# M = kv · wo in four 32-column strips on TensorE, in a linear-attention and MLP block

## The chip, the cores and the metric

One core of a Trainium2 chip. The metric is the time of one execution in device microseconds (us); a profiled execution also gives a trace, whose span is some 2 us shorter than the time (221.4 us for the 223.35 us of the profiled run before). On one core a run counts as slow when it is over 1.5% above the fastest of its kernel; ratios use fast runs only. The first run of the kernel before (255.02 us) is such an outlier; its other two are 223.43 and 223.21 us.

## The reference, cut to what matters

```python
# x: 2048 tokens x 640;  H = 32 heads of 20
xn  = layernorm(x)
q, k, v = split(xn @ wqkv)                       # per head
pq, pk = phi(q), phi(k)                          # phi(t) = (t + 1 if t > 0 else exp(t)) + 1e-6
kv  = einsum("bhsd,bhse->bhde", pk, v)           # 20 x 20 per head
num = einsum("bhqd,bhde->bhqe", pq, kv)
den = einsum("bhqd,bhd->bhq", pq, sum_s(pk)) + 1e-6
A   = (num / den) @ wo
B   = gelu(xn @ w1 + b1) @ w2 + b2
out = x + A + B
```

The kernel never forms `num`. It folds `kv` (block diagonal over heads, 640 x 640) into `wo` once, M = kv · wo, and then computes A as (pq / den) · M. The change is in the making of M.

## The kernel before

A small planner writes one instruction list per engine in program order and adds semaphore waits where a tile or a PSUM bank is written, read or reused. Its PSUM tensor (`ps` in the traces, which all matmuls shown here write to) is allocated and used as eight banks of 512 fp32 per partition; `take(n)` hands them out in a ring, so **who used a bank last decides what a group of matmuls waits for**.

```python
def take(n):                      # ring over the 8 PSUM banks; pairs start at an even bank
    b = ring[0]
    if n == 2 and b % 2: b += 1
    b %= 8
    ring[0] = (b + n) % 8
    return b
...
def z_step():                     # z = sum of phi(k); ZB = head mask times z, for the denominator
    ...                           # ten one-column matmuls, a copy to z_sb
    for j in range(DT):           # DT = 5
        Pl.ins(v, lambda e, j=j: e.tensor_scalar(ZB[:, j, :], bmask[:], z_sb[:, j:j + 1], None, ALU.mult), ...)

def kvt_step():                   # kv transposed, off-head entries masked to zero by VectorE
    for t in range(DT):
        b = take(1)
        ...
        Pl.ins(v, lambda e, b=b, t=t: e.tensor_tensor(
            out=KVT[:, t, e0[t]:e1[t]], in0=bank(b, 0, Wd[t]), in1=maskKV[t][:], op=ALU.mult), ...)

def m_step():
    for j in range(DT):
        b = take(2)
        fns = []
        for t in range(DT):
            for h in range(2):
                fns.append(lambda e, t=t, h=h, b=b, j=j: e.matmul(
                    bank(b + h, 0, HW), KVT[:, t, j:D:DT], Wo[:, t, h * HW:(h + 1) * HW],   # HW = 320
                    start=(t == 0), stop=(t == DT - 1)))
        Pl.ins("tensor", fns, reads=[r_KVT, r_Wo], writes=B_[b:b + 2])
        Pl.ins("scalar", lambda e, b=b, j=j: e.activation(halves(Msb[:, j, :]), pair(b), ACT.Copy), ...)

def den_step(c):                  # denominator of one chunk of 512 tokens
    b = take(1)
    ...                           # five matmuls ZB x PQ; then VectorE: add, reciprocal, five multiplies

q_chunk(0)                        # five units: five matmuls of 512 columns, exp on ScalarE, phi on VectorE
z_step()
kvt_step()
q_chunk(1)
m_step()
den_step(0)
q_chunk(2)
q_chunk(3)
...
for t in range(NT):               # 16 output tiles, with the other denominators in between
    out_tile(t)
```

Each of M's five groups (one per j) takes every fifth column of KVT, 128 in all, as the stationary operand, and multiplies it with five blocks of Wo in two halves of 320 columns: 10 matmuls. Most of each operand is zero. 32 of its 128 columns cover 160 channels, eight heads, whose values lie in only two of the five 128-row blocks of KVT.

Of the kernel before, what the change touches and what calls it, by code (L numbers as in the profile page):

```python
# [112 lines left out]
def bass_parallel_sum__linear_attn_block__dense_activation_gelu__prompt_kernel(  # L113
    nc: bass.Bass, A_x, A_wqkv, A_wo, B_x, B_w1, B_b1, B_w2, B_b2, out):
    Batch, S, D = A_x.shape
# [6 lines left out]
    DT = D // P  # L122
# [3 lines left out]
    HW = D // 2  # L126
# [10 lines left out]
    with contextlib.ExitStack() as es:  # L137
# [14 lines left out]
        KVT = W1f[:, DT * D:2 * DT * D].rearrange("p (k d) -> p k d", k=DT)  # L152
        Wqkv = sb("Wqkv", [P, DT, 3 * D], BF16)
        W2 = sb("W2", [P, JT, D], BF16)
        Wo = sb("Wo", [P, DT, D], BF16)
# [28 lines left out]
        def take(n):  # L184
            b = ring[0]
            if n == 2 and b % 2:
                b += 1
# [4 lines that stand above are left out]
        def bank(b, lo=0, hi=512):  # L192
            return ps[:, b * 512 + lo: b * 512 + hi]

        def pair(b):
            return ps[:, b * 512:(b + 2) * 512].rearrange("p (a n) -> p a n", a=2)[:, :, 0:HW]

        def halves(ap):
            return ap.rearrange("p (a n) -> p a n", a=2)
# [222 lines left out]
        for t in range(NT):  # L422
            b = take(2)
            fns = []
# [10 lines left out]
        for f in range(DT):  # L435
            b = take(2)
# [51 lines left out]
        def m_step():  # L488
            for j in range(DT):
                b = take(2)  # L490
                fns = []
                for t in range(DT):
                    for h in range(2):
                        fns.append(lambda e, t=t, h=h, b=b, j=j: e.matmul(  # L494
                            bank(b + h, 0, HW), KVT[:, t, j:D:DT], Wo[:, t, h * HW:(h + 1) * HW],
                            start=(t == 0), stop=(t == DT - 1)))
                Pl.ins("tensor", fns, reads=[r_KVT, r_Wo], writes=B_[b:b + 2])
                Pl.ins("scalar", lambda e, b=b, j=j: e.activation(halves(Msb[:, j, :]), pair(b), ACT.Copy),
                       reads=B_[b:b + 2], writes=[r_M[j], r_zsum, r_zhl])
# [25 lines left out]
# [5 lines that stand above are left out]
# [83 lines left out]
```

## Time and profile before

| | before |
|---|---|
| time, median (of the first three runs, the outlier included) | 223.43 us |
| span of the trace | 221.4 us |
| TensorE (PE) busy | 214.4 us, 97% |
| M: first matmul to the denominator's first | 6.79 us |
| denominator's first to first output tile | 12.3 us |
| first output tile to the end | 80.2 us |

A note on the denominator. In all of these traces this denominator has four matmul records, not five, and it is the first that has none: the four run on to the next q chunk without a gap. I take its start as 0.22 us (one 512-column matmul) before the first one recorded, here 129.19 - 0.22 = 128.97.

From the page of the profile: the span, busy times with shares and instruction counts, PE's busy share in 40 slices in tenths, its granted clock in tenths, and the chain that ended last by engine.

```profile
span 221.4 us, 3944 instructions
PE 214.4 (97%) x1603; PEld 148.6 (67%) x1612; DVE 125.8 (57%) x227; ACT 74.3 (34%) x140; POOL 41.7 (19%) x74
PE   7699999999999999999999999999999999999994
PEclk9999999999999999999999999999999999999999
PE 88%; DVE 5%; DMA 3%; SPq 1%; issue 1%; DVEq 0%
```

PE is the limit nearly everywhere (97% busy, 88% of the chain that ended last), at full clock (mean granted clock 1.000). The timeline of PE around M (start us, duration us, engine, line, operation, output <- inputs, shapes, count):

```profile
117.01 5.34 PE L460 MATMUL ps<-xnT,Wqkv 128*128 128x512 bf16 x24
122.19 6.96 PE L494 MATMUL ps<-Wo,W 128*128 128x320 bf16 x50
129.19 1.03 PE L504 MATMUL ps<-PQ,ZB 128*128 128x512 bf16 x4
130.06 10.95 PE L460 MATMUL ps<-xnT,Wqkv 128*128 128x512 bf16 x49
141.27 3.42 PE L548 MATMUL ps<-W,HG 128*128 128x320 bf16 x24 [0.26 <-DVE PQ L417]
```

M is the second row: 50 matmuls, one every 136 ns, with no pause. (Its 6.96 us include the 0.17 us by which the last matmul outlasts its spacing.)

VectorE (DVE) in the same stretch. L415 and L417 are the phi of the second q chunk, L507 and L509 the denominator:

```profile
120.12 0.28 DVE L415 TENSOR_SCALAR ek<-ek 128x512 bf16<-128x512 bf16 x1
...
124.50 0.69 DVE L417 SCALAR_TENSOR_TENSOR PQ<-ps,ek 128x512 bf16<-128x512 f32 x1
130.26 0.69 DVE L507 TENSOR_SCALAR den_sb<-ps 128x512 f32<-128x512 f32 x1 [5.07 <-PE ps L504]
130.98 3.35 DVE L509 RECIPROCAL rden<-den_sb 128x512 bf16<-128x512 f32 x1
```

VectorE finishes that phi at 125.19, late, one unit per us, and then idles 5.07 us.

### The profile page before, as it was taken

To read this page: it belongs to the slowest core of one execution; us is meant where nothing else is said; L and a number is where in the kernel's file an instruction comes from. 1 tells how busy PE (TensorE), PEld (TensorE's weight loads), DVE (VectorE), ACT (ScalarE), POOL (GpSimd) and SP (SyncE) were. 2 spreads that over 40 slices of the span, in tenths; PEclk is the share of its full clock that TensorE was granted. 3 is DMA by queue.
4 is the path that set the end of the run, shared out by engine and by line. 5 is a ranking of instruction groups with operands and counts; after the bars stand their busy time and mean duration, and the time that the engine had idled before them with its cause. 6 is when DMAs were issued, how large, how long until landed. Compare 5 with 4: busy or idle time off the path is not lost.

```text
span 221.4 us, 3944 instructions
## 1 busy us (share of the span) xinstructions
PE 214.4 (97%) x1603; PEld 148.6 (67%) x1612; DVE 125.8 (57%) x227; ACT 74.3 (34%) x140; POOL 41.7 (19%) x74
## 2 busy tenths in 40 slices
PE   7699999999999999999999999999999999999994
PEld 2489999544447777777665865567767776777773
DVE  2767778500004888899078549889929414811211
ACT  2378877566667555111254542600000000000000
POOL 2246554200000000000000000079993000000000
PEclk9999999999999999999999999999999999999999
DMA  5999960000000000000000000254520010010011
GB/s 156 340 363 364 362 233 0 1 3 0 0 0 0 3 0 3 0 0 3 0 0 1 3 0 0 66 173 119 170 70 30 30 60 32 0 62 30 30 46 47
DMA packets 13706, 15.50 MB, mean 70 GB/s; under 512 B 632, under 2 KB 13688, under 8 KB 13688
## 3 DMA queue, kind: packets, MB, share of 16 engines
q1 hardware_dynamic: 13688, 15.24, 21.1%
q8 instruction: 13, 0.21, 0.4%
q14 instruction: 5, 0.04, 0.1%
HBM read 12.62 MB, written 2.62 MB: 69 GB/s over the span
## 4 chain that ended last, share of the span: by engine, by line
PE 88%; DVE 5%; DMA 3%; SPq 1%; issue 1%; DVEq 0%
PE ps L548 33%; PE ps L350 23%; PE ps L438 10%; PE ps L427 10%; PE ps L460 5%; PE ps L494 3%; DMA xPK<-in_A_x_dram 3%; PE ps L504 2%; PE ps L334 2%; DVE PQ L417 2%; DVE rden L509 2%; DVE PQ L511 1%; SPq L235 1%; PE ps L480 1%; SPq L231 1%
## 5 line engine op out<-in xcount | busy, mean ns | idle before, releaser
L350 PE MATMUL ps<-xnT,W 128*128 128x128 bf16 (+2 forms) x447 | 54.8, 279 | 2.1 <-DVE xnT L342 1.9
L548 PE MATMUL ps<-W,HG 128*128 128x320 bf16 x384 | 54.9, 299 | 0.3 <-DVE PQ L417 0.3
L548 PEld LDWEIGHTS ps<-W,HG 128*128 128x128 bf16 x384 | 37.5, 98 | 15.7 <-issue 0.7
L350 PEld LDWEIGHTS ps<-xnT,W 128*128 128x128 bf16 x450 | 36.1, 98 | 17.1 <-DVE xnT L342 1.5
L354 ACT ACTIVATE HG<-ps,b1c 128x128 bf16<-128x128 f32 (+2 forms) x90 | 41.1, 489 | 18.9 <-PE ps L350 17.5
L520 POOL TENSOR_TENSOR xnT<-xnT,b2bc 128x640 bf16<-128x640 bf16 x16 | 22.6, 1448 | 102.1 <-DMA xnT<-in_A_x_dram 102.1
L554 DVE TENSOR_TENSOR out_sb<-ps,xnT 128x640 bf16<-128x640 f32 x15 | 12.3, 823 | 33.4 <-PE ps L548 31.6
L414 ACT ACTIVATE ek<-ps 128x512 bf16<-128x512 f32 (+1 forms) x36 | 23.2, 645 | 23.8 <-PE ps L427 9.2
L415 DVE TENSOR_SCALAR ek<-ek 128x512 bf16<-128x512 bf16 (+1 forms) x36 | 10.9, 304 | 30.7 <-ACT ek L414 29.5
L548 PE MATMUL ps<-Msb,PQ 128*128 128x320 bf16 x160 | 24.5, 299 | 0.0
L427 PE MATMUL ps<-Wqkv,xnT 128*128 128x320 bf16 x160 | 21.9, 299 | 0.0
L438 PE MATMUL ps<-xPK,xn_tm 128*128 128x320 bf16 x160 | 21.9, 299 | 0.0
L460 PE MATMUL ps<-xnT,Wqkv 128*128 128x512 bf16 x97 | 21.6, 379 | 0.2
L427 PEld LDWEIGHTS ps<-Wqkv,xnT 128*128 128x128 bf16 x160 | 15.7, 98 | 6.2
L548 PEld LDWEIGHTS ps<-Msb,PQ 128*128 128x128 bf16 x160 | 15.7, 98 | 6.1
L438 PEld LDWEIGHTS ps<-xPK,xn_tm 128*128 128x128 bf16 x160 | 15.7, 98 | 6.1
L460 PEld LDWEIGHTS ps<-xnT,Wqkv 128*128 128x128 bf16 x100 | 11.7, 117 | 9.5
L307 DVE BATCH_NORM_STATS2 stats<-xPK 128x6 f32<-128x320 bf16 x32 | 15.1, 471 | 4.4 <-DMA xPK<-in_A_x_dram 4.4
L417 DVE SCALAR_TENSOR_TENSOR PQ<-ps,ek 128x512 bf16<-128x512 f32 x20 | 13.8, 692 | 2.1
L417 DVE SCALAR_TENSOR_TENSOR xPK<-ps,ek 128x640 bf16<-128x640 f32 x16 | 13.2, 825 | 1.7
L509 DVE RECIPROCAL rden<-den_sb 128x512 bf16<-128x512 f32 x4 | 13.4, 3353 | 0.1
L511 DVE TENSOR_TENSOR PQ<-PQ,rden 128x512 bf16<-128x512 bf16 x20 | 12.2, 674 | 0.1
(50 smaller groups left out, 113.6 us busy)
## 6 DMA issues: line engine op xcount, KB each, us to landing
xnT<-in_A_x_dram SPq DMA_DIRECT2D x4, 640.0 KB, 4.4
Wqkv<-in_A_wqkv_dram SPq DMA_DIRECT2D x3, 800.0 KB, 12.0
out_dram<-out_sb SPq DMA_DIRECT2D x15, 160.0 KB, 1.8
W<-in_B_w_dram SPq DMA_DIRECT2D x4, 480.0 KB, 5.7
xPK<-in_A_x_dram SPq DMA_DIRECT2D x3, 640.0 KB, 8.6
W<-in_B_w_dram SPq DMA_DIRECT2D x1, 1920.0 KB, 14.2
Wo<-in_A_wo_dram SPq DMA_DIRECT2D x1, 800.0 KB, 10.7
xPK<-in_A_x_dram SPq DMA_DIRECT2D x4, 160.0 KB, 4.8
```

The costliest lines, as they stand in the source:

```text
L307: Pl.ins(v, lambda e: e.bn_stats(stats[:, s, 6 * h:6 * h + 6], x_in[:, t, h * HW:(h + 1) * HW]), reads=[r_x[t]], writes=[r_stats[s]])
L350: Pl.ins("tensor", [(lambda e, k=k: e.matmul(bank(b, 0, w), W1[:, k, jb * P:(jb + 1) * P], xnT[:, k, tok], start=(k == 0), stop=(k == DT - ...
L354: Pl.ins("scalar", lambda e: e.activation(HG[:, jb, tok], bank(b, 0, w), ACT.Gelu_apprx_tanh, bias=b1c[:, jb:jb + 1]), reads=[B_[b], r_b1c ...
L414: Pl.ins("scalar", lambda e: e.activation(e2, src, ACT.Exp), reads=br, writes=[r_ek[s]])
L417: Pl.ins(v, lambda e: e.scalar_tensor_tensor(out=d2, in0=src, scalar=0.0, in1=e2, op0=ALU.max, op1=ALU.add), reads=br + [r_ek[s]], writes= ...
L427: fns.append(lambda e, k=k, h=h, b=b, t=t: e.matmul(bank(b + h, 0, HW), xnT[:, k, t * P:(t + 1) * P], Wqkv[:, k, D + h * HW:D + (h + 1) * ...
L438: Pl.ins("tensor", [(lambda e, t=t, h=h, b=b, f=f: e.matmul(bank(b + h, 0, HW), xn_tm[:, t, f * P:(f + 1) * P], PK[:, t, h * HW:(h + 1) * ...
L460: Pl.ins("tensor", [(lambda e, k=k, j=j, b=b: e.matmul(bank(b), Wqkv[:, k, j:D:DT], xnT[:, k, cc], start=(k == 0), stop=(k == DT - 1))) fo ...
L509: Pl.ins(v, lambda e: e.reciprocal(rden[:], den_sb[:]), reads=[r_den], writes=[r_rden])
L511: Pl.ins(v, lambda e, j=j: e.tensor_tensor(out=PQ[:, j, cc], in0=PQ[:, j, cc], in1=rden[:], op=ALU.mult), reads=[r_rden, r_PQ[c][j]], writ ...
L520: Pl.ins(g, lambda e: e.tensor_tensor(out=x_res[:, t, :], in0=x_res[:, t, :], in1=b2bc[:], op=ALU.add), reads=[r_xr[t // CH], r_b2], write ...
L548: return lambda e: e.matmul(bank(b + h, 0, HW), seq[i][0], seq[i][1][:, h * HW:(h + 1) * HW], start=(i == 0), stop=(i == n - 1))
```

## The change

The intent is to skip the zero blocks. Each group is cut into four quarters q of 32 columns. A quarter needs only blocks q and q+1, and its output goes to its own strip of 32 PSUM partitions. The hope is that four matmuls, one for each strip, then run at once; no trace before the change shows that.

```diff
-                for t in range(DT):
-                    for h in range(2):
-                        fns.append(lambda e, t=t, h=h, b=b, j=j: e.matmul(
-                            bank(b + h, 0, HW), KVT[:, t, j:D:DT], Wo[:, t, h * HW:(h + 1) * HW],
-                            start=(t == 0), stop=(t == DT - 1)))
+                for h in range(2):
+                    for i in range(2):
+                        for q in range(4):
+                            c0 = j + 32 * DT * q
+                            fns.append(lambda e, t=q + i, q=q, i=i, h=h, b=b, c0=c0: e.matmul(
+                                bank(b + h, 0, HW)[32 * q:32 * q + 32, :],
+                                KVT[:, t, c0:c0 + 31 * DT + 1:DT], Wo[:, t, h * HW:(h + 1) * HW],
+                                start=(i == 0), stop=(i == 1)))
```

That is 80 matmuls in place of 50, each with 320 moving columns. Everything else stays, in the same order on every engine.

## The prediction

> **What bounds the kernel now.** TensorE: busy 214.4 of 221.4 us (97%), full clock throughout (the page, parts 1 and 2), and 88% of the chain that ended last is PE (part 4). M is one stretch of that chain: 50 matmuls of 320 columns, 122.35 to 129.14 us, 6.79 us, 136 ns each. So at most 6.8 us (3.0%) can be won.
>
> **What the change does.** Each of the five M groups (one per j) has 16 matmuls with a 32-column stationary operand instead of 10 with 128 columns: 80 instead of 50, all of 320 moving columns. One by one at 136 ns, M would take 10.9 us, 4.1 us longer. The change pays only if four neighbours, which write four different 32-partition strips of PSUM, run at once. [...] Two floors for a group: streaming, four matmuls per strip, 4 x 136 = 0.54 us; issue, 16 pairs of weight load and matmul, and the ten one-column matmuls that sum z go by in 0.36 us in the chain, 36 ns a pair, so 0.58 us. [...] I expect 0.7 us a group (0.55 to 1.0) against 1.36.
>
> Nothing else moves: the order of instructions is the same on every engine.
>
> **What is on the critical path.** Five groups of 0.7 would be 3.5 us, but M will stop being a pure TensorE stretch. Its groups take PSUM pairs in a ring. The third and fourth pair are those of the second q chunk's last four units, which VectorE frees: in the timeline it is behind (after the KVT masking) and does one unit per us, the third until 123.2, the fifth until 125.19. So the fourth group cannot start before about 125.3 (a release takes 0.14 us to reach PE, as at the first output tile). Two groups[...] later, about 126.8, the denominator matmul starts, against 129.19 now. The fifth group needs ScalarE's copy of the first, done by about 124: no wait. Of the 3.3 us of PE work removed, some 1 us becomes a new wait, and about 2.3 us remain.
>
> Are they kept? From the denominator to the first output tile, PE (1.03 + 50 x 0.216 = 11.8 us) and VectorE (0.70 + 3.35 + 1.77 + five phi units of 1.0 = 10.8 us) both start from that matmul, so both shift whole; so do the reloads of x, released by the last q matmul. The output stage is PE-bound (68.45 of 71.4 us). I expect the whole shift at the end.
>
> **Prediction:** 223.43 - 2.3 = 221.1 us, range 220.4 to 222.4. Faster by over 2%: 0.01; within 2%: 0.95; slower by over 2%: 0.04.
>
> **What would show it.** 80 matmuls in M with starts in bunches of four, a group of about 0.7 us; PE waiting for VectorE's phi before M's fourth group, about 1 us, and briefly before the third; the denominator matmul at 126.3 to 127.5; VectorE's wait before it 5.1 -> about 2.7 us; first output tile near 139, the rest unchanged and earlier.
>
> **What would make it wrong.** The column tiles don't overlap, or each weight load waits for the matmul before it: M then takes 10.9 to 13 us and the kernel 227 to 230. Or issue costs over 80 ns a matmul: M takes 6.5 us and nothing is won. If groups take under 0.6 us, VectorE's release caps the win near 2.8 us.

Passages that no run of this case shows are cut from the text above, a term of its sum among them: 0.17 us, my estimate (299 less 136 ns, both from the trace before) for a pause at each end of M, where TensorE switches between matmuls of 128 stationary columns ("full array" below) and strips. With it the denominator's start came to 125.3 + 2 x 0.7 + 0.17, about 126.8 us; without it, it is 126.7. The 2.3 us won and the 221.1 us are those of the whole sum. The 0.7 us a group was my estimate, above the two floors of 0.54 and 0.58 us.

## The result, and the profile after

The changed kernel's median is 220.82 us (220.43 to 221.26, four runs). Ratios here are the mean time of one kernel's fast runs over that of the other's in the same rounds, so they are not quite ratios of the medians: 0.989, 95% interval 0.9866 to 0.9914, 1.1% faster. The means are 220.83 and 223.29, a difference of 2.46 us.

The page of the changed kernel, the same rows:

```profile
span 218.7 us, 4004 instructions
PE 210.3 (96%) x1633; PEld 144.8 (66%) x1642; DVE 125.6 (57%) x227; ACT 74.3 (34%) x140; POOL 41.8 (19%) x74
PE   7699999999999999999999799999999999999994
PEclk9999999999999999999999999999999999999999
PE 82%; DVE 11%; DMA 3%; SPq 1%; issue 1%; ACT 0%; DVEq 0%
```

A dent of 7 has appeared in PE's row, and VectorE's share of the chain has gone from 5% to 11%. PE's timeline shows where (L496 is M, L507 the denominator):

```profile
116.72 5.34 PE L460 MATMUL ps<-xnT,Wqkv 128*128 128x512 bf16 x24
122.00 1.83 PE L496 MATMUL ps<-Wo,W 128*32 128x320 bf16 x48
125.05 1.29 PE L496 MATMUL ps<-Wo,W 128*32 128x320 bf16 x32 [1.22 <-DVE PQ L417]
126.50 1.03 PE L507 MATMUL ps<-PQ,ZB 128*128 128x512 bf16 x4 [0.16 <-issue]
127.36 10.95 PE L460 MATMUL ps<-xnT,Wqkv 128*128 128x512 bf16 x49
138.56 3.42 PE L551 MATMUL ps<-W,HG 128*128 128x320 bf16 x24 [0.25 <-DVE PQ L417]
```

M is now two pieces: three groups in one go, a pause, and two groups. The pause ends when VectorE's last phi of the second q chunk does:

```profile
124.21 0.69 DVE L417 SCALAR_TENSOR_TENSOR PQ<-ps,ek 128x512 bf16<-128x512 f32 x1
127.56 0.69 DVE L510 TENSOR_SCALAR den_sb<-ps 128x512 f32<-128x512 f32 x1 [2.66 <-PE ps L507]
```

That phi ends at 124.90 and the fourth group starts at 125.05. The bracket's 1.22 us counts from the end that the profile gives to the previous matmul. Counted from when the next bunch would have started (136 ns after the last one, at 123.67), PE lost 1.38 us. The row of the weight loads names ScalarE's copy of M (L501) as the last releaser instead; e5 and e6 below decide between the two.

To see the strips at work, count matmuls that touch equal stretches of 0.54 us, four times 136 ns (stretch us, its length, PE busy and count, weight loads and count, clock, DMA). Before:

```profile
122.19:122.73 0.54, 0.54 (x5) 0.47 (x4) 1.00 0.00 0
125.00:125.54 0.54, 0.54 (x6) 0.47 (x5) 1.00 0.00 0
```

After:

```profile
122.00:122.54 0.54, 0.54 (x16) 0.51 (x20) 1.00 0.00 0
122.54:123.08 0.54, 0.54 (x24) 0.45 (x20) 1.00 0.00 0
```

The first stretch of each has no predecessors in flight: 16 matmuls now start where 4 did (the fifth of x5 touches the very end). Single records show them in bunches of four, 1 to 5 ns apart, one bunch every 136 ns (after the pause one strip runs some 33 ns ahead of the other three). A group takes 4 x 136 ns = 0.54 us instead of 1.36.

| interval (us) | before | after | changed kernel, second profile |
|---|---|---|---|
| M to denominator | 6.79 | 4.29 | 4.31 |
| denominator to first output tile | 12.3 | 12.3 | 12.3 |
| first output tile to end | 80.16 | 80.15 | 80.16 |

So what M gave up was kept to the end. The spans differ by 2.7 us because this execution also reached M's q chunk 0.29 us earlier (117.01 against 116.72). Such shifts before M differ from run to run (117.37 in e1, 117.11 in e2). From that q chunk to the denominator 2.40 us were won.

### The profile page after: what moved, and what is told of

Read it like the earlier page. It is cut to its first block, busy times and chain, and to the rows that moved or that the text cites. A ratio compares the mean times of both kernels' runs of the same rounds, so it can differ in the third digit from the quotient of the medians.

```text
span 218.7 us, 4004 instructions
## 1 busy us (share of the span) xinstructions
PE 210.3 (96%) x1633; PEld 144.8 (66%) x1642; DVE 125.6 (57%) x227; ACT 74.3 (34%) x140; POOL 41.8 (19%) x74
## 4 chain that ended last, share of the span: by engine, by line
PE 82%; DVE 11%; DMA 3%; SPq 1%; issue 1%; ACT 0%; DVEq 0%
PE ps L551 34%; PE ps L350 23%; PE ps L438 10%; PE ps L427 10%; DVE PQ L417 5%; DMA xPK<-in_A_x_dram 3%; PE ps L507 2%; PE ps L334 2%; DVE ek L415 2%; DVE rden L512 2%; DVE PQ L514 1%; SPq L235 1%; DVE W L484 1%; SPq L231 1%; DVE ZB L474 1%
## 5 line engine op out<-in xcount | busy, mean ns | idle before, releaser
L415 DVE TENSOR_SCALAR ek<-ek 128x512 bf16<-128x512 bf16 (+1 forms) x36 | 10.9, 303 | 30.7 <-ACT ek L414 29.5
```

The costliest lines, as they stand in the source:

```text
L415: Pl.ins(v, lambda e: e.tensor_scalar(et, et, 1.0, 1e-6, ALU.min, ALU.add), reads=[r_ek[s]], writes=[r_ek[s]])
```

## The experiments

Twelve kernels ran, each correct unless said otherwise. Times scatter: in some rounds runs counted as fast are 1 to 3 us longer than the rest, the kernel before included (222.97 to 225.66 in one set). Every "denominator to first output tile" is 12.28 to 12.29 us except in e11, and every "output to end" 80.15 to 80.17. So the interval from M to the denominator is the sharper measure. Of the experiments' runs, all those over 1.3 us above the fastest of their set have a mean granted TensorE clock of 0.991 to 0.993 of full speed, and all others, within 1.03 us of it, 0.998 to 1.000. The profile of e7 caught one (225.78 us): its clock is 0.70 between 11.2 and 16.8 us, M starts 2.4 us later than in the kernel before, and the span is 2.4 us longer. So that run's excess lies before M, outside the intervals used here.

After the result I first assumed theory A: the strips work at once, but matmuls start in program order.

### e1: strip as the outermost loop

```diff
-                for h in range(2):
-                    for i in range(2):
-                        for q in range(4):
+                for q in range(4):
+                    for h in range(2):
+                        for i in range(2):
```

> Same 80 matmuls of 32 columns, same result, but with the strip as outermost loop: four neighbours go to the same strip. Theory A (strips run at once, but matmuls start in program order, each when the one before it has started and its own strip is free): 12 x 136 ns = 1.63 us a group and a few ns, M from its first matmul to the denominator's first about 8.3 us (after: 4.29), no wait for VectorE before the fourth group, kernel about 224.8 us, slower than before. Theory B (strips are independent, order does not matter): group 0.54 us, 220.8 us. Theory C (no overlap at all is needed, a 32-column matmul is just cheaper, some 34 ns each): 0.54 us, 220.8 us. If nothing overlapped: 2.18 us a group, 227.5 us.

Measured: 220.97 us (220.38 to 221.41), M to denominator 4.34 us against 4.29. Theory A falls. The matmul counts of e1 in its first 0.54 us stretches:

```profile
122.64:123.18 0.54, 0.54 (x16) 0.54 (x17) 1.00 0.00 0
123.18:123.72 0.54, 0.54 (x24) 0.52 (x17) 1.00 0.00 0
```

They are those of the changed kernel. Starts within a bunch are now 12 to 14 ns apart in the first five bunches, instead of 1 to 5 (later bunches are less even). With the strip outermost, the first matmuls of two strips lie four pairs of load and matmul apart in the program, and 13/4 is the 3 to 4 ns of one pair in the changed kernel. So the picture became, as an estimate from these two spacings: a pair's turn comes every 3 to 4 ns in program order, and a strip that is busy for its 136 ns does not hold up the others. Across strips the starts do not keep to program order: four starts lie within 3 x 13 = 39 ns and one strip alone takes a matmul only every 136 ns (e9), so the 5th, 9th and 13th matmuls of the program must have started before the second.

### e2: the half as the innermost loop

```diff
-                for h in range(2):
-                    for i in range(2):
-                        for q in range(4):
+                for i in range(2):
+                    for q in range(4):
+                        for h in range(2):
```

> The same 80 matmuls with the half (h) as innermost loop: two neighbours to one strip, then the next strip. Theory A (in-order start, strip busy for 136 ns): 8 x 140 ns = 1.12 us a group, M 5.7 us, no wait for VectorE, kernel about 222.3 us, so over half of the gain is lost by loop order alone. Theories B and C: 0.54 us a group, 220.8 us.

Measured: 220.96 us, M to denominator 4.29 us, starts 7, 7 and 6 ns apart in the first bunch (two pairs) and mostly 4, 10 and 4 in the next ones. Theory A falls here too. B or C remain. Neighbours of one strip now go to two different banks in turn, and each bunch still holds four, so it is not a shared bank that keeps a strip to one matmul per 136 ns.

### e3: twice as many matmuls of half the width

```diff
+                for h, u in ((0, 0), (0, 1), (1, 0), (1, 1)):
...
+                                bank(b + h, u * HW // 2, (u + 1) * HW // 2)[32 * q:32 * q + 32, :],
+                                KVT[:, t, c0:c0 + 31 * DT + 1:DT],
+                                Wo[:, t, h * HW + u * HW // 2:h * HW + (u + 1) * HW // 2],
```

> Each matmul split in two of 160 moving columns: 32 a group, same work. If the strips' streaming sets the 0.54 us of a group (theory A), bunches of four now come every 69 ns and a group stays near 0.55 us, kernel 220.8 us. If issue sets it (my 36 ns a pair from the z sum, or the 17 ns per instruction that the after trace shows), a bunch still takes 136 to 144 ns, a group 1.09 to 1.15 us, M 5.6 us and the kernel about 222.1 us.

Measured: 221.74 us median (runs of 220.75, 220.80, and, at the lower clock, 222.68 and 223.53), M to denominator 4.30 us, bunches of four every 69 ns. The columns that each strip streams set the time (136 ns for 320, 69 ns for 160), not the handing out. My 36 ns per pair, taken from the z sum, is no floor here: a pair went by every 69/4 = 17 ns.

### e4: two strips of 64 columns

```diff
-                    for i in range(2):
-                        for q in range(4):
-                            c0 = j + 32 * DT * q
+                    for i in range(3):
+                        for q in range(2):
+                            c0 = j + 64 * DT * q
...     # t = 2 * q + i; output partitions 64 * q to 64 * q + 63; stop at i == 2
```

> Two strips of 64 columns in place of four of 32: 12 matmuls a group, 6 in each strip. Theory A (time = matmuls in the fullest strip x 136 ns): 6 x 136 = 0.82 us a group; third group free, fourth still waits for VectorE (0.6 us), denominator 0.5 us later than after, kernel about 221.3 us. Without overlap: 12 x 136 = 1.63 us a group, about 224.7 us. Theory C (cost goes with the operand's columns): 12 x 68 = 0.82, not told apart here.

Measured: 221.69 us median, M to denominator 4.86 us, 0.57 more than the changed kernel (0.5 expected). Starts come in twos every 136 ns, six per group. The rule "matmuls of the fullest strip times 136 ns" holds. Four strips need four, two strips need six.

### e9: everything to one strip (wrong result)

```diff
-                                bank(b + h, 0, HW)[32 * q:32 * q + 32, :],
+                                bank(b + h, 0, HW)[0:32, :],
...
-                                start=(i == 0), stop=(i == 1)))
+                                start=True, stop=True))
```

> Wrong result on purpose: the 80 matmuls of 32 columns all write to the first strip of 32 partitions, each a group of its own; everything else as in the changed kernel. After e1 and e2, theory B (strips are four queues of their own, one matmul at a time in each): 16 x 136 ns = 2.17 us a group, M about 11 us, kernel about 227.5 us. Theory C (a 32-column matmul is cheap wherever it goes, no strips needed): bunches of four every 136 ns again, 220.8 us.

Measured: 227.74 us, ratio 1.0219 (1.0193 to 1.0246), slower than before, though not by a clear 2%. PE's timeline of e9, and its matmul count in the first 0.54 us of M:

```profile
122.40 11.06 PE L496 MATMUL ps<-Wo,W 128*32 128x320 bf16 x80
133.62 1.03 PE L507 MATMUL ps<-PQ,ZB 128*128 128x512 bf16 x4 [0.16 <-issue]
```

```profile
122.40:122.94 0.54, 0.54 (x4) 0.48 (x5) 1.00 0.00 0
```

The same 80 matmuls take 136 ns each when they share a strip: 4 in a stretch that held 16. Theory C is out. A 32-column matmul is not cheaper than a 128-column one (136 ns each here and in the kernel before; their weight loads are recorded at 113 and 117 ns); the whole gain is that four run at once. This is also the failure that the prediction feared, now with its price: M would have taken 11.0 us.

### e10: twenty matmuls in a row to each strip

```diff
-                for h in range(2):
-                    for i in range(2):
-                        for q in range(4):
+                for q in range(4):
+                    for h, i in 5 * [(0, 0), (0, 1), (1, 0), (1, 1)]:
+                        if True:
```

> The right result, with the strip outermost as in e1 and the four matmuls of a strip done five times over, so 20 in a row go to one strip and 80 make a group. It asks how far ahead matmuls are handed to the strips. If far enough for all four strips (48 pairs of load and matmul or more, or 16 waiting in each strip): 20 x 136 = 2.72 us a group, M 13.6 us, kernel about 230.3 us. If 32 pairs in program order: some 3.7 us a group, M 18.3 us, about 235 us. If 16 to 20 pairs: 5.45 us a group, about 244 us. If each strip holds only 4 and a full one stops the rest: 8.2 us a group, about 257 us.

Measured: 261.41 us. M's 400 matmuls take 44.92 us, which the timeline of e10 shows in one row:

```profile
121.96 44.92 PE L496 MATMUL ps<-Wo,W 128*32 128x320 bf16 x400
```

That is about 8.8 us a group, 2.21 us per strip of twenty, where full overlap would give 2.7 us a group and none 10.9, so about three quarters of the overlap is gone. The last of the expected cases was nearest (8.2 us, 257 us). The single records show where the overlap that is left lies. At each of the 19 borders between runs, the next strip's first matmul starts 5 to 7 ns after the old strip's 17th, while three of the old strip's are still to start; between these short overlaps one strip starts alone, one matmul every 136 ns. Around the first border 10 matmuls touch the stretch from 124.17 to 124.71 us, and only 6 the one from 125.00 to 125.54, as many as in the kernel before. So of a run of twenty only the last three overlap with the next run, while e1's four in a row kept full speed (4.34 us from M to the denominator). What holds the next strip back until then was not shown. My 8.2 us a group amounts to four times 15 slots of 136 ns from one strip's start to the next's; measured are some 16 (2.21 us).

### e5: other PSUM banks for M

Strips explain M's own speed. The 1.38 us pause was the second question.

```diff
+        forced = []                    # banks to hand out before the ring goes on
...
         q_chunk(1)
+        forced += [0, 2, 4, 0, 2]      # M (the ring gives 0, 2, 4, 6, 0)
+        forced += [6] + [7, 4, 5, 0, 1] + [2, 3, 6, 7, 4] + [0, 5, 2]
         m_step()
```

> The changed kernel with other PSUM banks for M (pairs 0, 2, 4, 0, 2 in place of 0, 2, 4, 6, 0) and a list for what follows, so that M's fourth group waits for ScalarE's copy of the first (done at 123.5) and not for VectorE's last phi of q (124.9). My theory (the 1.4 us before the fourth group is a wait for VectorE's release of the bank and nothing else): M runs in one piece, 2.72 us and two switches of 0.1, the denominator starts 1.4 us earlier, kernel 220.8 - 1.4 = 219.4 us. Rival 1 (the wait is TensorE's own, or VectorE would hold up the denominator anyway, as it is behind): the denominator's evaluation cannot start earlier, gain under 0.3 us. Rival 2 (the wait is for ScalarE's copies of M): no change or worse, as the fourth group now needs one.

Measured: 219.67 us median (219.22 to 221.26), M to denominator 3.04 us, 1.24 less than with the ring. PE's timeline of e5:

```profile
122.25 3.10 PE L502 MATMUL ps<-Wo,W 128*32 128x320 bf16 x80
125.51 1.03 PE L513 MATMUL ps<-PQ,ZB 128*128 128x512 bf16 x4 [0.16 <-issue]
```

M is one piece again. The pause was a wait for the bank and nothing else, and the denominator did start earlier, so rival 1 falls. Rival 2 has a small part: the last group starts 0.27 us after the bunch before it, not 0.13, which fits ScalarE's second copy of M, done near 124.5. That is the missing 0.14 of the 1.4 us.

### e6: the ZB multiplies on ScalarE

```diff
-                Pl.ins(v, lambda e, j=j: e.tensor_scalar(ZB[:, j, :], bmask[:], z_sb[:, j:j + 1], None, ALU.mult),
+                Pl.ins("scalar", lambda e, j=j: e.activation(ZB[:, j, :], bmask[:], ACT.Copy, scale=z_sb[:, j:j + 1]),
```

> The changed kernel with the five ZB multiplies (1.41 us on VectorE, right before the KVT masking) moved to ScalarE, which idles 2.4 us there; banks as in the changed kernel. My theory: VectorE frees the fourth group's banks 1.1 us earlier, then bound by the q chunk's own pace (last phi ends near 123.8), the wait shrinks from 1.4 to about 0.3 us, kernel about 219.7 us. Rival 2 (ScalarE's copies are the gate): no change. Rival: ScalarE's work delays its exp of q by over 0.3 us and eats it.

Measured: 220.56 us median, M to denominator 3.70 us, so 0.59 us won where 1.1 was expected. The wait before the fourth group is shorter and still ends with VectorE's last phi (at 124.49):

```profile
124.64 1.29 PE L496 MATMUL ps<-Wo,W 128*32 128x320 bf16 x32 [0.62 <-DVE PQ L417]
```

ScalarE's timeline in e6 shows why no more was won:

```profile
116.77 2.14 ACT L474 ACTIVATE ZB<-bmask,z_sb 128x128 bf16<-128x128 bf16 x5 [1.23 <-DVE z_sb L472]
118.81 1.06 ACT L414 ACTIVATE ek<-ps 128x512 bf16<-128x512 f32 x2
```

The five multiplies cost ScalarE 2.14 us where VectorE needed 1.41, and its exp of q began at 118.81 instead of about 118.0, so VectorE got its input later. The direction confirms VectorE's release as the gate (if ScalarE's copies were the gate, nothing would have changed); half the size was eaten by the rival that I had named.

### e7: the kernel before with e5's banks

The same bank lists, put into the kernel before.

> The kernel before with the bank list of e5. In the kernel before the fourth group starts at 126.3, after VectorE's release at 125.2, so my theory says that nothing is gained: 223.3 us (within 0.3). If the bank list is good for something else (the later stages), it shows here as a gain of its own, to be taken off e5.

Measured: 223.34 us against 223.25 us, ratio 0.9988 (0.9953 to 1.0023), M to denominator 6.79 us as before. The bank list has no value of its own. The wait that it removes exists only once M is fast. (The profile is that of the one long run, 225.78 us; the other six took 223.02 to 223.41 us.)

### e8: the price of switching between strips and the full array

```diff
                 fns = []
+                fns.append(lambda e, b=b: e.matmul(bank(b, 0, 1)[0:128, :], warm[:, 0:128], warm[:, 0:1],
+                                                   start=True, stop=True))
```

> e5 with one extra one-column matmul of the full 128 columns before each of the five groups, into the bank that the group then overwrites: eight more switches between full array and strips inside M. From the gaps of 0.09 and 0.11 us at the ends of M I expect 0.1 us a switch, so 0.8 us more in M (0.2 us at each of four borders), plus some 0.04 us for each extra matmul: denominator 0.8 to 1.1 us later than in e5. If a switch costs nothing and the gaps have another cause (the semaphore, the first weight load), only the extra matmuls' 0.2 us shows.

Measured: 220.26 us median; M's first group to the denominator takes 3.84 us against 3.04 in e5, 0.79 more, just under the expected 0.8 to 1.1. PE's timeline of e8:

```profile
122.06 0.75 PE L504 MATMUL ps<-Wo,W 128*32 128x320 bf16 x16
122.74 0.18 PE L498 MATMUL ps<-warm 128*128 128x1 bf16 x1
122.84 0.75 PE L504 MATMUL ps<-Wo,W 128*32 128x320 bf16 x16
123.52 0.18 PE L498 MATMUL ps<-warm 128*128 128x1 bf16 x1
123.63 0.75 PE L504 MATMUL ps<-Wo,W 128*32 128x320 bf16 x16
```

Groups start every 0.79 us instead of 0.54: two switches and one tiny matmul cost 0.24 us (0.03 of it is a late second bunch, which every start of M on strips shows), so about 0.1 us a switch, as the gaps at M's ends suggested. This e8 did not isolate the tiny matmul's own share.

### e11 and e12: a version that beats both, and the changed kernel again

e11 is e5 with one more reordering of banks, aimed at the wait before the first output tile.

```diff
-        forced += [6] + [7, 4, 5, 0, 1] + [2, 3, 6, 7, 4] + [0, 5, 2]
+        forced += [6] + [7, 4, 0, 1, 5] + [2, 3, 6, 7, 4] + [0, 5, 2]
```

> e5 with the third q chunk's units on banks 7, 4, 0, 1, 5 in place of 7, 4, 5, 0, 1, so that the first output tile's pair (0, 1) is freed by VectorE one unit (1.0 us) sooner. In all runs so far PE waits 0.25 us there for VectorE's phi; if that is all, the output stage starts 0.25 us earlier: kernel 0.25 us under e5, about 219.4 us, and faster than before by 1.7%. If the wait only moves to the following denominator, nothing.

> The changed kernel unaltered, to compare with e11 on the same chip: 220.8 us, den matmul 4.29 us after M's first as in its first profile.

Measured on one chip: e11 219.62 us median (219.31 to 221.40), ratio to before 0.9867 (0.9835 to 0.9899); the changed kernel again 220.68 us, ratio 0.9887 (0.9875 to 0.9900). In the trace e11 has 3.04 us from M to the denominator and 11.87 us from there to the first output tile, 0.42 less than every other kernel; PE's timeline has no wait in front of that tile any more:

```profile
137.13 3.42 PE L559 MATMUL ps<-W,HG 128*128 128x320 bf16 x24
```

The win is 0.42 us and not 0.25, because the bracket's 0.25 had counted from the modelled end of the last q matmul, 0.17 us after its slot was over. By the trace e11 is 1.27 + 0.42 = 1.7 us ahead of the changed kernel, by the medians 1.06 us. Two of e11's six runs, near 221.3, have the lower granted clock (0.992); the other four, 219.31 to 219.88 us, lie below all four of the changed kernel's (220.60 to 220.84). The 219.4 us expected for e11 fits them; e5 and e11 were not run on the same chip.

## Why the prediction was right

The predicted 221.1 us met 220.82, and the 2.3 us to be won met 2.40 us in the trace. Point by point:

- **The strips overlap** (0.7 us a group, range 0.55 to 1.0): right in kind, too cautious in size. A group took 0.54 us, four full streams at once, just under the range. The mis-sized term is the issue cost: 36 ns a pair came from ten matmuls with 128-column loads, and e3 ran pairs every 17 ns. In the steady stream of four, e9 against the changed kernel shows 4.0x (136 ns a matmul against 136 ns a bunch).
- **A new wait on VectorE before the fourth group** (about 1 us): right, and e5 and e6 show it by taking it away. It was 1.38 us, larger because the groups were faster. The brief wait foreseen before the third group did not come: its banks were released at 122.91, and it started near 123.1 in step.
- **Switches**: estimated 0.17 us at each end, measured 0.09 and 0.11 (and 0.24 in e8 for two switches and a one-column matmul). What TensorE does in these gaps was not shown.
- **The sum.** Streaming fell from 50 to 20 slots of 136 ns, -4.07 us. Against that stand 1.38 of waiting and 0.20 of switches, -2.49 in all; the trace shows -2.40, and a late second bunch after each of M's two starts takes some 0.06 of the rest. My 2.3 was right partly by luck. I had compared with 129.19, the second denominator matmul, as the first has no record; the true start was 128.97. That error of 0.22 and groups that were too slow nearly cancelled. The prediction's own side case, "if groups take under 0.6 us, VectorE's release caps the win near 2.8 us", is the one that came. Less the same 0.22 and, if it left out the switch after M, the 0.11 of that, its 2.8 becomes some 2.5.
- **The whole shift is kept**: right. From the denominator to the first output tile it is 12.28 to 12.29 us in both kernels and in eleven of the twelve experiments, e9 and e10 included, where M is much longer; e11 alone changed it, on purpose.
- **Markers.** VectorE's idle time before the denominator was predicted near 2.7 us and is 2.66. The first output tile was predicted near 139 and is at 138.56. The denominator was predicted between 126.3 and 127.5; its first recorded matmul is at 126.50, its first at 126.28, which is 126.57 with the 0.29 us earlier start taken out.

What was wrong was not in the prediction but in my first explanation of it: theory A, program-order starts across strips, died in e1 and e2.

Left open: what makes the pairs come 3 to 4 ns apart, what holds the next strip back in e10, and whether one semaphore on the last matmul in the program stays safe if strips finish in another order. The kernels here do that, and all but e9, which was wrong on purpose, gave right results. But the last starts of e1's four strips lie 0.1 us apart, the records do not say which strip is last, and no run tests a reader quick enough to notice.

## What to carry to other kernels

Before skipping zeros by narrow strips, count matmuls in the fullest strip and multiply by the streaming time of one (136 ns here for 320 columns, 69 ns for 160). The order among strips hardly mattered here with up to four in a row to the same one (4.29 us from M to the denominator, 4.34 in e1); with twenty in e10 a group took 8.8 us where full overlap would give 2.7, and nothing between was run. When a TensorE stretch becomes shorter, look up who last used each PSUM bank that it takes: here a third of the saved streaming time (1.38 of 4.07 us) went into a wait that another order of banks all but removed (0.14 us left in e5), and that same order was worth nothing to the kernel before.
